# Two of sixteen pairs of PSUM copies: the second half of each moved from ScalarE to VectorE

## The chip, the cores and the metric

The kernel runs on one core of a Trainium2 chip. The metric is device time in microseconds (us) of one launch, the median of several runs. One run was also profiled: its instructions on TensorE (PE, with its weight loads as PEld), VectorE (DVE), ScalarE (ACT), GpSimd (POOL) and SyncE (SP, which issues the DMAs) are on a trace whose times count from the first instruction.

## The reference

A 2048 by 512 input goes through two blocks. The first normalizes each row, takes a real 2-D Fourier transform, multiplies it with a complex filter, transforms back and adds the input. The second normalizes again and applies a gated GELU layer of width 1376. All of it is float32.

```python
def _A_ref(x, w_r, w_i):
    X = jnp.fft.rfft2(x, axes=(-2, -1))
    X = X * (w_r + 1j * w_i)
    return jnp.fft.irfft2(X, s=(S, D), axes=(-2, -1))

h  = x + _A_ref(_layernorm(x), A_w_r, A_w_i)
g, u = _layernorm(h) @ w_gate, _layernorm(h) @ w_up
h2 = h + (_gelu(g) * u) @ w_down
```

## The kernel before

The transforms are matmuls with tables of sines and cosines. The kernel goes through four stages. The first (to about 30 us in the trace) loads and normalizes the rows and does a first transform. The second is the **filter stage**, about 30 to 74 us, and holds the change. The third transforms back along the other axis, adds the input and begins the gated layer. The fourth is the rest of the gated layer, and takes most of the time.

The filter stage works on 16 tiles of 128 partitions, t = 0 to 15. A tile passes through these steps, each named by the letter that stands for it in the string `SECOND`, which lists all steps of the stage in the order in which every engine gets its instructions:

- `o` (function `over_d`, line 420): four matmuls (L425, 128x128, float32; the trace shows each as two passes, so eight PE rows) write the tile's row spectra into two of the eight PSUM banks: banks 6 and 7 for tile 0, 0 and 1 for tile 1, 2 and 3 for tile 2, then 0 and 1 or 2 and 3. ScalarE then copies them to an SBUF tile `dp`, in two instructions (L429): partitions 0 to 63 first, then partitions 64 to 127 with the two banks' halves read in reverse. Each is 64x512 float32.
- `f` (`filtered`, line 431): two matmuls with weights `cfs` (L437, 128x256, four PE rows) read `dp` and write two banks, 4 and 5 for an even tile, 6 and 7 for an odd one. VectorE multiplies them with the filter's real and imaginary parts `wt` in three operations from PSUM (L443, L444, L445, here called the tile's **triple**), and GpSimd adds the two products (L453, L454) to `z`. SP then issues the load of the filter of tile t+8.
- `p` (`patch_w`): a ScalarE copy of 8 columns into the loaded filter tile (L472). The triple of the same tile waits for it.
- `b` (`back`): four matmuls with `z` as weights (L464, eight PE rows) write bank 0 or 1; at the end ScalarE copies that bank to `gh` (L469).
- `h`: a step of preparing weights of the gated layer. ScalarE rounds a piece (L156) and GpSimd subtracts it (L157).

The string begins `h p0 o0.6 o1.0 h h o2.2 h p1 f0 f1 p2 o3.0 o4.2 h f2 o5.0 h p3 p4 f3 o6.2 o7.0 h f4 o8.2 p5 f5 p6 p7 b0 o9.2 f6 p8 p9 b1 f7 o10.2 h p10 f8`. The number behind the point is the first PSUM bank. An engine works through its own instructions strictly in this order, and waits at each until its inputs are there and the place that it writes is free. So `o4` cannot start before ScalarE has read tile 2 out of banks 2 and 3, and `f(t)` not before VectorE has finished the triple of tile t-2, which reads the same two banks.

Of the kernel before, what the change touches and what calls it, by code (L numbers as in the profile page):

```python
# [15 lines left out]
AF = mybir.ActivationFunctionType  # L16
# [13 lines left out]
BY_POOL = (3,)  # L30

BY_THEN = (8, 12, 9)

START = """
f0 s0 g0 r0 n0 s1 c0 v0 g1 s2 m3 q3 r1 g2 f1 v1 n1 r2 m5 c1 q5 n2 c2 m7 c3 f2 s4 s6 g4 a0 b0 w7 g6 v2 q7 r4 n4 m9 c4
# [84 lines left out]
def kernel(  # L120
# [16 lines left out]
    pe, act, dve, pool = nc.tensor, nc.scalar, nc.vector, nc.gpsimd  # L137
# [97 lines left out]
    with (  # L235
# [182 lines left out]
        dps, zs = {}, {}  # L418

        def over_d(t, k):  # L420

            pd = ps[:, k : k + 2]
            for c, (e, q) in enumerate(((0, 0), (1, 1), (0, 1), (1, 0))):
                o = pd[:, e, q * NQ // 2 :][:, :P]
                pe.matmul(o, ts[:, t, c].rearrange("p x b k -> p (x b k)"), dfs[:, c], start=True, stop=True)  # L425
            pdv = pd[:, :, :NQ].rearrange("p e (s q) -> p s e q", s=2)[:, :, :, :P]
            dps[t] = w2.tile([P, 2, 2, P], F32, name="dp", bufs=5)
            for h, d in ((slice(0, 64), 1), (slice(64, P), -1)):
                act.activation(dps[t][h], pdv[h, ::d], AF.Copy)  # L429

        def filtered(t):
            dp, wt = dps.pop(t), wts.pop(t)
# [41 lines left out]
        with tc.manual_schedule(engines={et.PE, et.Activation, et.DVE, et.Pool}):  # L474
            prep = itertools.chain(raw0, load_gu(1, True))
            with tc.issue_after(kept.ins):
                for m, op in enumerate((ALU.add, ALU.subtract)):
                    pool.tensor_tensor(wh[:, :, m], ws[:, 0, :, m], ws[:, 1, :, m], op=op)
                act.activation(wh, wh, AF.Copy, scale=0.5)
            for _ in range(4):  # L480
                next(prep)
            rounded = 0
            for op in SECOND.split():
                name, *place = op.split(".")
                t = int(name[1:] or 0)
                if name == "h":
                    for _ in range(2 if rounded == 6 else 1):
                        next(prep, None)
                    rounded += 1
                elif name[0] == "o":  # L490
                    over_d(t, int(place[0]))
                elif name[0] == "f":
                    filtered(t)
                    if t + AHEAD < NT:
                        load_w(t + AHEAD)
                else:
                    (patch_w if name[0] == "p" else back)(t)
# [469 lines left out]
    def late(b):  # L967

        if b not in BY_THEN:

            with held("lo"):
                unfolded(b, row())
        yield
        xt = row()
        behind(nc.sync.dma_start(xt, x3[:, b]), pooled["raw"])
        py = ps[:, next(bank_67)]
        pe.matmul(py, mis[:, b], gh[:, b], start=True, stop=True)  # L977
        dve.scalar_tensor_tensor(gh[:, b], xt, mv[:, b, 0:1], py, op0=ALU.subtract, op1=ALU.add)  # L978
        for _ in stats2(b):
            pass  # L980
        yield
# [261 lines left out]
    lates = {2: (9, 13), 3: (10,), 4: (14,), 5: (11,), 6: (15,)}  # L1243
    ending = [late(b) for b in BY_THEN[:2]]
    for g in ending:
# [185 lines left out]
```

## Time and profile before

| what | value |
|---|---|
| median of 3 runs | 440.24 us (440.03 to 440.96) |
| the profiled execution's own time | 440.57 us |
| its span, first to last instruction | 438.3 us |
| PE busy | 432.5 us, 99% of the span |
| DVE busy | 311.2 us, 71% |
| ACT busy | 244.3 us, 56% |
| POOL busy | 314.9 us, 72% |
| copies L429 on ACT | 32 instructions of 0.591 to 0.593 us |

A row of the timeline gives the start in us, the length in us, the engine, the line, the operation, the tile written and the tiles read, the shapes, and how many instructions were merged into the row. Behind it, in brackets, stands how long the engine had been idle and what ended that. Matmuls are pipelined: a pass that runs 0.275 us is followed by the next one after 0.11 us, so the distance from the start of one PE row to that of the next tells more than the row's length. The waits list gives, for pairs of engine and line, the total idle time, how often, and the longest.

### The profile page before, as it was taken

The numbers are of one execution on the slowest core, as the hardware profiler recorded it, in microseconds if no ns is written. First come the engines' busy times: TensorE is split into PE (matmuls) and PEld (weight loads), VectorE is DVE, ScalarE is ACT, GpSimd is POOL, SyncE is SP. The second block draws the span as 40 slices with busy tenths as digits, with TensorE's granted clock in tenths as the row PEclk, the third lists the DMA queues.
The fourth block names the chain that finished last, engine by engine and source line by source line (L and its number), as shares of the span: only waits on it lengthen the run. The fifth ranks groups of instructions, "written<-read, shape, count | busy, mean of one in ns | idle before, by whom it ended". The sixth has DMA issues, their size and how long they took to land.

```text
span 438.3 us, 6627 instructions
## 1 busy us (share of the span) xinstructions
PE 432.5 (99%) x2275; PEld 367.0 (84%) x2275; DVE 311.2 (71%) x576; ACT 244.3 (56%) x505; POOL 314.9 (72%) x346
## 2 busy tenths in 40 slices
PE   8999999999999999999999999999999999999996
PEld 8998999789978777877888888888888888888885
DVE  5968976798764766368734579578677786687786
ACT  5989785799912442124432787376455653565640
POOL 6987897999958788658653944067879779787821
PEclk9999999999999999999999999999999999999999
DMA  8996904320032112112220203501212021200005
GB/s 265 404 414 118 357 12 150 134 72 25 1 120 97 49 55 91 48 49 72 72 73 24 73 25 120 169 15 58 73 48 73 28 69 49 72 25 2 0 1 194
DMA packets 23542, 41.60 MB, mean 95 GB/s; under 512 B 4178, under 2 KB 9810, under 8 KB 23380
## 3 DMA queue, kind: packets, MB, share of 16 engines
q1 hardware_dynamic: 23220, 40.92, 27.6%
q8 instruction: 18, 0.29, 0.3%
q10 hardware_dynamic: 288, 0.26, 0.2%
q14 instruction: 16, 0.13, 0.1%
HBM read 36.97 MB, written 4.20 MB: 94 GB/s over the span
## 4 chain that ended last, share of the span: by engine, by line
PE 92%; POOL 4%; DMA 1%; issue 1%; DVE 1%; ACT 0%; SPq 0%; DVEq 0%
PE ps L163 16%; PE ps L165 16%; PE ps L164 16%; PE ps L769 14%; PE ps L1108 11%; PE ps L425 4%; PE ps L530 3%; PE ps L437 3%; PE ps L464 3%; POOL pn L339 2%; POOL pn L338 2%; PE ps L869 2%; PE ps L977 1%; PE ps L1214 1%; DMA gh<-in_x 1%
## 5 line engine op out<-in xcount | busy, mean ns | idle before, releaser
L163 PE MATMUL ps<-cb,gu 128*128 128x512 f32 (+1 forms) x336 | 127.4, 379 | 0.0
L165 PE MATMUL ps<-cb,gu 128*128 128x512 f32 (+1 forms) x336 | 124.9, 372 | 0.0
L164 PE MATMUL ps<-cb,gu 128*128 128x512 f32 (+1 forms) x336 | 124.8, 371 | 0.0
L673 ACT ACTIVATE s<-ps 128x512 f32<-128x512 f32 (+1 forms) x72 | 40.3, 561 | 87.4 <-PE ps L165 87.2
L228 POOL TENSOR_TENSOR gu<-raw,gu 128x768 fp32r<-128x768 f32 (+1 forms) x42 | 61.4, 1481 | 29.9 <-DVE gu L223 15.5
L164 PEld LDWEIGHTS ps<-cb,gu 128*128 128x128 f32 x336 | 63.3, 188 | 11.8 <-issue 1.0
L163 PEld LDWEIGHTS ps<-cb,gu 128*128 128x128 f32 x336 | 63.3, 188 | 11.7 <-issue 1.0
L165 PEld LDWEIGHTS ps<-cb,gu 128*128 128x128 f32 x336 | 63.2, 188 | 11.1
L769 PE MATMUL ps<-wd,a 128*128 128x512 f32 x264 | 63.6, 393 | 0.0
L769 PEld LDWEIGHTS ps<-wd,a 128*128 128x128 f32 x264 | 49.2, 188 | 11.5 <-DVE gh L978 1.0
L682 DVE TENSOR_TENSOR ps<-ps,s 128x512 f32<-128x512 f32 (+1 forms) x48 | 31.2, 652 | 27.4 <-PE ps L165 25.3
L1115 DVE TENSOR_TENSOR gh<-ps,gh 128x512 f32<-128x512 f32 x66 | 44.2, 681 | 1.0 <-PE ps L1108 1.0
L679 ACT ACTIVATE s<-s 128x512 f32<-128x512 f32 (+1 forms) x48 | 28.5, 594 | 20.9 <-DVE s L676 20.9
L775 DVE TENSOR_TENSOR gh<-ps,gh 128x512 f32<-128x512 f32 x24 | 16.5, 689 | 27.0 <-PE ps L769 26.9
L676 DVE TENSOR_TENSOR s<-ps,s 128x512 f32<-128x512 f32 (+1 forms) x48 | 30.8, 641 | 5.8 <-PE ps L165 4.7
L511 POOL TENSOR_TENSOR wd<-wdr,wd 128x512 fp32r<-128x512 f32 x12 | 15.6, 1296 | 18.6 <-ACT wd L509 18.6
L676 DVE TENSOR_TENSOR ps<-ps,s 128x512 f32<-128x512 f32 (+1 forms) x24 | 15.7, 653 | 16.8 <-ACT s L673 16.6
L1021 POOL TENSOR_TENSOR t<-mis,t 128x768 fp32r<-128x768 f32 (+1 forms) x9 | 13.3, 1481 | 13.2 <-ACT t L1019 13.1
L688 ACT ACTIVATE a<-ps 128x512 fp32r<-128x512 f32 (+1 forms) x26 | 13.7, 532 | 15.6 <-DVE ps L682 15.6
L429 ACT ACTIVATE dp<-ps 64x512 f32<-64x512 f32 x32 | 18.9, 592 | 4.0 <-PE ps L425 3.6
L207 POOL TENSOR_TENSOR raw<-raw 128x256 f32<-128x256 f32 x16 | 11.8, 737 | 12.9 <-DMA raw<-in_wgu 11.2
L453 POOL TENSOR_TENSOR z<-t,t 128x520 f32<-128x520 f32 x15 | 19.4, 1296 | 2.1 <-DVE t L445 2.1
(183 smaller groups left out, 898.1 us busy)
## 6 DMA issues: line engine op xcount, KB each, us to landing
wt<-in_w SPq DMA_DIRECT2D x16, 520.0 KB, 7.1
raw<-in_wgu SPq DMA_DIRECT2D x32, 256.0 KB, 3.0
out<-gh SPq DMA_DIRECT2D x15, 256.0 KB, 2.0
gh<-in_x SPq DMA_DIRECT2D x7, 512.0 KB, 9.5
row<-in_x SPq DMA_DIRECT2D x12, 256.0 KB, 2.7
wdr<-in_wd SPq DMA_DIRECT2D x12, 256.0 KB, 2.6
mis<-in_wd SPq DMA_DIRECT2D x10, 256.0 KB, 2.6
a<-in_wgu SPq DMA_DIRECT2D x8, 256.0 KB, 3.1
```

The source lines that it names most:

```text
L163: pe.matmul(o, lh, rh, start=(i == 0 and not onto), stop=False, skip_group_check=True)
L164: pe.matmul(o, lh, rl, start=False, stop=False, skip_group_check=True)
L165: last = pe.matmul(o, ll, rh, start=False, stop=(i == n - 1), skip_group_check=True)
L228: pooled["lo"] = pool.tensor_tensor(r[:, 1, m], t[:, m], r[:, 0, m].bitcast(F32), op=ALU.subtract)
L453: eng.tensor_tensor(z[:, :, first], t1[:, :, first], t2[:, :, first], op=ALU.add)
L673: return lambda: act.activation(to, a, AF.Copy)
L676: return lambda: dve.tensor_tensor(to, a, b, op=ALU.add)
L679: return lambda: act.activation(g, g, AF.Gelu_apprx_tanh)
L682: return lambda: dve.tensor_tensor(u, u, g, op=ALU.mult)
L769: pe.matmul(o, parts_of[tiles.index((0, f))][:, ha, i // 4, r], wds[f][:, hw, c], start=start, stop=stop)
L1108: pe.matmul(ps[:, k], w[:, hw], a[ha], start=start and hw + ha == 0, stop=hw == 1, skip_group_check=True)
L1115: by.tensor_tensor(to, o, to, op=ALU.add)
```

## The change

For tiles 0 and 1 alone, the second of the two copies out of PSUM (partitions 64 to 127) is a `tensor_copy` on VectorE. The first copy of these two tiles and both copies of the other fourteen stay on ScalarE.

```diff
+COPIED_BY_VECTOR = (0, 1)
...
             for h, d in ((slice(0, 64), 1), (slice(64, P), -1)):
-                act.activation(dps[t][h], pdv[h, ::d], AF.Copy)
+                if t in COPIED_BY_VECTOR and d < 0:
+                    dve.tensor_copy(dps[t][h], pdv[h, ::d])
+                else:
+                    act.activation(dps[t][h], pdv[h, ::d], AF.Copy)
```

The changed program has five lines more, so L429 becomes L434 on ScalarE and L432 on VectorE, L437 becomes L442, L443 to L445 become L448 to L450, L472 becomes L477 and L156 becomes L158. Names in brackets are what an instruction waits for: an engine's counter, or a DMA queue (DMAHW).

ScalarE at the head of the filter stage, before (`gu` is the rounding of step `h`, `wt` the patch `p`, `dp` the copies):

```order
L472 ACTIVATE wt<-wh 128x4x2 [waits DMAHW2_49,Activation_49]
L429 ACTIVATE dp<-ps 64x512 [waits DVE_49,PE_49]
L429 ACTIVATE dp<-ps 64x512
L429 ACTIVATE dp<-ps 64x512 [waits DVE_49,PE_49]
L429 ACTIVATE dp<-ps 64x512
L156 ACTIVATE gu<-raw 128x256
L156 ACTIVATE gu<-raw 128x256 [waits Pool_49]
L429 ACTIVATE dp<-ps 64x512 [waits PE_49]
L429 ACTIVATE dp<-ps 64x512
L156 ACTIVATE gu<-raw 128x256 [waits DMAHW1_49]
```

The same place now:

```order
L477 ACTIVATE wt<-wh 128x4x2 [waits DMAHW2_49,Activation_49]
L434 ACTIVATE dp<-ps 64x512 [waits DVE_49,PE_49] x2
L158 ACTIVATE gu<-raw 128x256
L158 ACTIVATE gu<-raw 128x256 [waits Pool_49]
L434 ACTIVATE dp<-ps 64x512 [waits PE_49]
L434 ACTIVATE dp<-ps 64x512
L158 ACTIVATE gu<-raw 128x256 [waits DMAHW1_49]
```

Four copies ahead of the two `gu` have become two, the first halves of tiles 0 and 1. Everything behind them stands as it did.

VectorE at the same place, before (`t` are the products of the triples):

```order
L383 COPY ts<-ps 128x16x4x4 [waits PE_49]
L412 TENSOR_SCALAR mv<-m_113 128x6
L443 TENSOR_TENSOR t_494<-ps,wt 128x520 [waits DVE_49,DMAHW2_49,PE_49,Activation_49]
L444 SCALAR_TENSOR_TENSOR t_495<-ps,wt 64x520
L445 TENSOR_TENSOR t_495<-ps,wt 64x520
```

And now:

```order
L385 COPY ts<-ps 128x16x4x4 [waits PE_49]
L414 TENSOR_SCALAR mv<-m_113 128x6
L432 COPY dp<-ps 64x512 [waits DMAHW5_49,DMAHW0_49,Activation_49]
L432 COPY dp<-ps 64x512 [waits Activation_49]
L448 TENSOR_TENSOR t_494<-ps,wt 128x520 [waits DMAHW2_49,PE_49]
L449 SCALAR_TENSOR_TENSOR t_495<-ps,wt 64x520
L450 TENSOR_TENSOR t_495<-ps,wt 64x520
```

The two copies stand ahead of the first triple. Each waits for ScalarE's counter: the value is the one reached when ScalarE has finished the first half of the same tile, not merely when PE has finished the matmuls. The two halves of a tile therefore still follow one another. On PE, the `f` matmuls of tiles 0 and 1 now wait for VectorE's counter where they waited for ScalarE's.

## The prediction

> **What bounds the kernel now.** I read first the page's chain of waits (the work that ended last, by engine), then the waits list for 30 to 75 us.
>
> ```profile
> PE 92%; POOL 4%; DMA 1%; issue 1%; DVE 1%; ACT 0%; SPq 0%; DVEq 0%
> ...
> PEld ps L425 <- ACT dp L429: 0.8, 4, 0.2
> ```
>
> PE carries the chain almost alone, so only time in which PE stands still, or starts later, can be gained. In the filter stage it stands still for the copies of the change (`dp`, L429): four times ahead of an `o`. The list shows only idle time above the overlap of the passes, so I read the timeline of PE row by row (start, length, line, passes).
>
> ```profile
> 30.29 2.92 PE L425 MATMUL ps<-dfs,ts 128*128 128x128 f32 x24
> ...
> 33.05 2.01 PE L437 MATMUL ps<-dp,cfs 128*128 128x256 f32 x8
> 34.89 2.16 PE L425 MATMUL ps<-dfs,ts 128*128 128x128 f32 x16
> 36.89 1.03 PE L437 MATMUL ps<-dp,cfs 128*128 128x256 f32 x4
> 37.76 1.16 PE L425 MATMUL ps<-dfs,ts 128*128 128x128 f32 x8
> 38.75 1.03 PE L437 MATMUL ps<-dp,cfs 128*128 128x256 f32 x4
> 39.62 2.18 PE L425 MATMUL ps<-dfs,ts 128*128 128x128 f32 x16
> 41.63 1.03 PE L437 MATMUL ps<-dp,cfs 128*128 128x256 f32 x4
> 42.51 1.16 PE L425 MATMUL ps<-dfs,ts 128*128 128x128 f32 x8
> 43.51 1.03 PE L437 MATMUL ps<-dp,cfs 128*128 128x256 f32 x4
> 44.37 1.05 PE L464 MATMUL ps<-cis,z 128*128 128x128 f32 x8
> 45.39 1.16 PE L425 MATMUL ps<-dfs,ts 128*128 128x128 f32 x8
> 46.39 1.03 PE L437 MATMUL ps<-dp,cfs 128*128 128x256 f32 x4
> ...
> 49.01 1.05 PE L425 MATMUL ps<-dfs,ts 128*128 128x128 f32 x8
> 49.99 1.13 PE L437 MATMUL ps<-dp,cfs 128*128 128x256 f32 x4
> ...
> 54.50 1.06 PE L425 MATMUL ps<-dfs,ts 128*128 128x128 f32 x8
> 55.40 1.03 PE L437 MATMUL ps<-dp,cfs 128*128 128x256 f32 x4
> 56.26 1.05 PE L464 MATMUL ps<-cis,z 128*128 128x128 f32 x8
> ...
> 68.62 5.76 PE L464 MATMUL ps<-cis,z 128*128 128x128 f32 x48
> ```
>
> An undisturbed `o` (eight L425 passes) takes 0.90 us from start to start (54.50 to 55.40), an `f` 0.86 (55.40 to 56.26); `b` has eight passes as well and is taken like `o`. Against that: f0+f1 took 34.89-33.05 = 1.84, 0.12 too long; o3+o4 2.00, 0.20 too long; o5 0.99, 0.09; o6+o7 2.01, 0.21; o8 1.00, 0.10; b0 1.02, 0.12; o9 1.00, 0.10; o10, up to the start of f8, 0.98, 0.08. That is 1.02 us of hidden stalls before f8 at 49.99. From there to 68.62 lie eight `f`, five `o` and eight `b`: 6.88+11.70 = 18.58 of 18.63 us. So behind f8 PE runs without gaps worth naming, and everything before f8 decides. What PE waited for is seen in ScalarE's timeline, and in a stretch of it by engine (columns: length, then busy us of PE, PEld, DVE, ACT, POOL).
>
> ```profile
> 31.46 2.41 ACT L429 ACTIVATE dp<-ps 64x512 f32<-64x512 f32 x4 [0.25 <-PE ps L425]
> 33.90 0.72 ACT L156 ACTIVATE gu<-raw 128x256 fp32r<-128x256 f32 x2
> 34.64 1.20 ACT L429 ACTIVATE dp<-ps 64x512 f32<-64x512 f32 x2
> 35.86 0.42 ACT L156 ACTIVATE gu<-raw 128x256 fp32r<-128x256 f32 x1
> 36.19 0.30 ACT L472 ACTIVATE wt<-wh 128x8 f32<-128x8 f32 x2
> 36.51 2.42 ACT L429 ACTIVATE dp<-ps 64x512 f32<-64x512 f32 x4
> 38.95 0.42 ACT L156 ACTIVATE gu<-raw 128x256 fp32r<-128x256 f32 x1
> ...
> 40.94 0.30 ACT L472 ACTIVATE wt<-wh 128x8 f32<-128x8 f32 x2
> ...
> 45.36 0.41 ACT L472 ACTIVATE wt<-wh 128x8 f32<-128x8 f32 x3
> ```
>
> ```profile
> 39.00:44.00 5.00, 5.00 (x35) 4.42 (x34) 4.39 (x7) 4.84 (x11) 4.50 (x7) 1.00 0.73 171
> ```
>
> ScalarE is the engine that is late: four copies in a row from 31.46, then `h`, and from 36.51 it works almost without a break (4.84 of 5 us). VectorE comes next; its rows for the first operation of tiles 0, 1, 3, 5 and 6, and the last operation of tile 6:
>
> ```profile
> 34.17 0.70 DVE L443 TENSOR_TENSOR t<-ps,wt 128x520 f32<-128x520 f32 x1 [3.34 <-ACT dp L429]
> ...
> 36.42 0.70 DVE L443 TENSOR_TENSOR t<-ps,wt 128x520 f32<-128x520 f32 x1
> ...
> 41.22 0.70 DVE L443 TENSOR_TENSOR t<-ps,wt 128x520 f32<-128x520 f32 x1 [0.53 <-POOL gu L157]
> ...
> 45.67 0.70 DVE L443 TENSOR_TENSOR t<-ps,wt 128x520 f32<-128x520 f32 x1 [0.17 <-issue]
> ...
> 47.82 0.70 DVE L443 TENSOR_TENSOR t<-ps,wt 128x520 f32<-128x520 f32 x1
> ...
> 49.25 0.69 DVE L445 TENSOR_TENSOR t<-ps,wt 64x520 f32<-64x520 f32 x1
> ```
>
> Triples that follow one another are 2.15 apart (45.67 to 47.82), and a triple ends 2.12 after its start (49.25+0.69 = 49.94). f8 starts 0.05 later, at 49.99: it writes the banks that triple 6 reads, so **f8 waits for VectorE**. VectorE's chain from 34.17 to 49.94 is 15.77 long, and seven triples back to back would need 6 x 2.15 + 2.12 = 15.02. The rest, 0.75, was lost where a triple waited. Triple 3 (idle 0.53) started right behind the patch p3, on ScalarE at 40.94 and done 0.20 later; the name in the bracket is of work that had ended by then, and I take p3. Triple 5 started 0.31 behind the start of p5 (45.36).
>
> **The change, part by part.** Two copies of 0.60 leave ScalarE and two come to VectorE. The trace has a copy from PSUM on VectorE only with 256 elements:
>
> ```profile
> L383 DVE COPY ts<-ps x1: 425/425/425, 29.8 to 29.8; 128x256 f32<-128x256 f32 x1
> ```
>
> The operations of the triples, 520 elements from PSUM, take 0.70. In line between 0.425 for 256 and 0.70 for 520, a copy of 512 takes **0.69 us**; I take that, and keep 0.43 and 0.70 as ends.
>
> *Tile 0.* ScalarE's half ends at 31.46+0.59 = 32.05. VectorE's copy waits for that; with 0.05 for the semaphore it runs from 32.10 to 32.79, where ScalarE's ended at 32.65. It is 0.14 later, and free: f0 could not start before PE had finished o2, which it did at 33.05. The cover is 0.2 us, and VectorE itself was idle (3.34 us ahead of 34.17). Behind the waiting copies VectorE has triple 0, which needs f0's result anyway and stays at 34.17. The filter load that SP issues behind triple 0 stays too.
>
> *Tile 1.* The third eight of the 24 passes end at 33.21, so o1's end at 32.31. ScalarE is now free and copies the first half at 32.35 to 32.95, VectorE the second at 33.00 to 33.69. f1, straight behind f0 at 33.91, finds it done. The 0.12 at f1 is gained and o3 starts at 34.77.
>
> *ScalarE.* The two `gu` run 32.95 to 33.69 (0.74, as 33.90 to 34.64), tile 2's copies to 34.91 (1.22), the next `gu` with p1 and p2 to 35.56 (0.65). Tile 3's copies need o3, done 34.77+1.06 = 35.83 (a row of o5, 1.16, less its 0.10 stall); so they start at 35.87, not 36.51. **ScalarE is 0.64 ahead**, the rest of its 1.2 us is lost in waiting for o3. From there it stays 0.64 ahead as long as PE is in time: tile 6's copies at 40.62 need o6, done 40.51 below; tile 8's at 43.50 need o8, done 43.17. So p3 starts at 40.30, p5 at 44.72.
>
> *PE.* o4 at 35.67 finds its banks copied (34.91): 0.20 gained. f2 36.57, o5 37.43 (banks copied by 37.08): 0.09 gained. f3 could start at 38.33, but its banks are read by triple 1, which now starts at 34.17+2.15 = 36.32, ends at 38.44, and lets f3 go at 38.49, with another 0.10 inside the stalled group, as o5 showed. Here **VectorE takes over the wait**, and most of the lead is gone for the moment: 38.75 before. Then o6 39.45, o7 40.35 (copied by 39.97), f4 41.25, o8 42.11 (41.84), f5 43.01, b0 43.87 (43.06), o9 44.77 (44.70, the tightest), f6 45.67, o10 48.29, and f8 could start at 49.19.
>
> *VectorE.* Triple 2 at 38.47, triple 3 at 40.62 (p3 done 40.50), triple 4 at 42.77, triple 5 behind p5 at 44.72+0.31 = 45.03, triple 6 at 47.18, done 49.30. f8 starts at 49.35 instead of 49.99: **0.64 us earlier**, and its inner stall stays.
>
> Behind f8 the stalls are small and each is a wait for work that PE itself started, so I carry the 0.64 through. The span becomes 438.3-0.64 = 437.7, the profiled execution's time 440.57-0.64 = 439.93. That execution lay 0.33 above the median; from the median I get 440.24-0.64 = **439.6 us**. If the copy takes 0.43, f0 still waits for PE and nothing changes; at 0.70 neither.
>
> **Rivals.**
> 1. *Hidden anyway.* If triple 3 does not move, because p3 or the triple waited for something else than ScalarE's turn, or if the lead is eaten in the later stages, little is left. With triple 3 fixed at 41.22, triple 4 is at 43.38, 5 at 45.53, 6 at 47.68, done 49.80; f8 at 49.85, gain 0.14: 440.1 us. For it: the bracket at 41.22 names another engine. Against: ScalarE had no break before p3. Chance 0.24.
> 2. *More.* VectorE's chain is at its shortest with 15.02: f8 at 34.17+15.02+0.05 = 49.24, and the 0.10 inside f8 gone as well. Gain 0.85: 439.4 us. It needs ScalarE 0.1 further ahead at p5, and nothing shows where from. Chance 0.12.
> 3. *Slower: the copies sit ahead of triple 0 in VectorE's queue.* If a copy takes D instead of 0.69, the second ends at 32.10+2D (from D = 0.9), and triple 0 starts behind it. f8 then starts 0.04+15.02+0.05 after that, and is later than 49.99 once 2D exceeds 2.78, so from D = 1.39 on; at D = 1.8 f8 starts at 50.81, 0.82 late: 441.1 us. Against it: no VectorE operation of this size from PSUM takes over 0.70 here. Chance 0.04.
> 4. *The copies wait for GpSimd.* GpSimd works back to back at this place:
>
> ```profile
> 31.68 0.73 POOL L215 TENSOR_TENSOR raw<-raw 128x256 f32<-128x256 f32 x1
> 32.37 0.73 POOL L157 TENSOR_TENSOR gu<-raw,gu 128x256 fp32r<-128x256 f32 x1
> ```
>
> If such a copy could not run beside GpSimd, the first would start at 33.10, behind the second row. With 0.69 it ends at 33.79, f0 starts at 33.84 instead of 33.05, triple 0 at 34.96, and f8 at 50.03: 440.3 us, no gain. Against it: triple 0 ran at its usual 0.70 from 34.17, and GpSimd's rows beside other VectorE work keep their 0.73. Chance 0.05.
>
> The Trainium skill has such a rule in SBUF — State Buffer, section "SBUF: two separate sides": a VectorE operation that uses both its SBUF ports and a GpSimd operation exclude one another for the whole instruction. But in VectorE: DVE Perf Modes, section "Why PSUM operands drop a tier", it says that a float32 operand in PSUM keeps an operation at one element per cycle, since there is one read port to PSUM; then no second port is taken and the lock does not apply. The row of L383, 425 ns for 256 elements, agrees with the single rate. By the second page the sum above holds, by the first alone rival 4 would.
>
> **How the numbers follow.** The forecast has 0.55. About 0.2% (0.88 us) is what a measurement of this kernel can tell from no change, and the forecast lies inside, as do rivals 1 and 4. Faster by over 0.2% means below 439.36: rival 2 lies at that edge and gives half of its 0.12, and the forecast gives 0.16 for steps sized too small and for runs that vary (440.03 to 440.96 above): 0.22. Slower than 441.12: half of rival 3, and 0.04 for variation and a later stage that answers badly: 0.06. Within: 0.72. The range goes from 439.0, rival 2 with 0.4 for variation, to 440.5, which takes in rivals 1 and 4; rival 3 stays out.
>
> **What would show it.** In the trace of the changed kernel: the two VectorE copies near 0.69 us, starting right behind ScalarE's halves; f0 still at 33.05 and triple 0 at 34.17; ScalarE's copies of tile 3 at about 35.9; no stall at o4, o5, o7 and o8, and a new one at f3 behind VectorE; triple 3 at about 40.6, f8 at about 49.35, and the first L530 row 0.64 before its old place. The prediction is wrong if a copy takes over 0.85, which would move f0; if triple 3 stays where it was; or if f8 is early and the end of the span is not.

## The result

| | before | after |
|---|---|---|
| median of 11 runs each | 440.24 us (439.92 to 440.96) | 439.29 us (439.12 to 439.69) |
| profiled execution, its span | 440.57, 438.3 us | 439.26, 437.0 us |
| first `o` to `f8` in the trace | 19.70 us | 19.04 us |
| first `o` to the first L530 row (now L535) | 44.16 us | 43.50 us |

The ratio is 0.998, with a 95% interval from 0.9973 to 0.9988. The kernel became 0.95 us faster, 0.22%; the prediction had 439.6, 0.64 us faster, and a range from 439.0 to 440.5. In the trace the filter stage is 0.66 us shorter. So the stage did what was worked out, and about 0.3 us of the gain came from elsewhere; the experiments look for it.

PE after the change, from the timeline (start, length, line, passes):

```profile
29.97 2.92 PE L427 MATMUL ps<-dfs,ts 128*128 128x128 f32 x24
32.72 1.89 PE L442 MATMUL ps<-dp,cfs 128*128 128x256 f32 x8
34.45 1.95 PE L427 MATMUL ps<-dfs,ts 128*128 128x128 f32 x16
36.23 1.03 PE L442 MATMUL ps<-dp,cfs 128*128 128x256 f32 x4
37.10 1.05 PE L427 MATMUL ps<-dfs,ts 128*128 128x128 f32 x8
38.12 1.13 PE L442 MATMUL ps<-dp,cfs 128*128 128x256 f32 x4
39.08 1.95 PE L427 MATMUL ps<-dfs,ts 128*128 128x128 f32 x16
...
49.01 1.13 PE L442 MATMUL ps<-dp,cfs 128*128 128x256 f32 x4
...
73.47 3.84 PE L535 MATMUL ps<-dis,gh 128*128 128x128 f32 x32
```

The stage begins 0.32 us earlier than in the trace of before, at 29.97 and not at 30.29. So places are compared from the first `o` on: `f0` 2.75 behind it in both, `f1` no longer late (f0 and f1 take 1.73 us together and not 1.84), `o3` and `o4` 1.78 instead of 2.00. From `o5` (37.10) to `f3` (38.12) it is 1.02 where an undisturbed `o` takes 0.90: the new stall of 0.12 ahead of `f3`. The row of `f3` is 1.13 us long, 0.10 longer than that of an undisturbed `f`, as that of `f8` is in both traces.

ScalarE and VectorE at the same place:

```profile
31.14 0.59 ACT L434 ACTIVATE dp<-ps 64x512 f32<-64x512 f32 x1 [0.26 <-PE ps L427]
32.03 0.59 ACT L434 ACTIVATE dp<-ps 64x512 f32<-64x512 f32 x1 [0.30 <-PE ps L427]
32.52 0.71 ACT L158 ACTIVATE gu<-raw 128x256 fp32r<-128x256 f32 x2
33.13 1.18 ACT L434 ACTIVATE dp<-ps 64x512 f32<-64x512 f32 x2
...
35.54 2.41 ACT L434 ACTIVATE dp<-ps 64x512 f32<-64x512 f32 x4 [0.58 <-PE ps L427]
```

```profile
31.76 0.69 DVE L432 COPY dp<-ps 64x512 f32<-64x512 f32 x1 [1.26 <-ACT dp L434]
32.65 0.69 DVE L432 COPY dp<-ps 64x512 f32<-64x512 f32 x1 [0.20 <-ACT dp L434]
33.79 0.70 DVE L448 TENSOR_TENSOR t<-ps,wt 128x520 f32<-128x520 f32 x1 [0.44 <-PE ps L442]
...
40.25 0.70 DVE L448 TENSOR_TENSOR t<-ps,wt 128x520 f32<-128x520 f32 x1
...
46.84 0.70 DVE L448 TENSOR_TENSOR t<-ps,wt 128x520 f32<-128x520 f32 x1
...
48.26 0.69 DVE L450 TENSOR_TENSOR t<-ps,wt 64x520 f32<-64x520 f32 x1
```

A copy takes 0.69 us on VectorE and 0.59 on ScalarE. VectorE's two copies lie in time in which it was idle before. ScalarE begins tile 3's copies 35.54-29.97 = 5.57 behind the first `o`; before it was 36.51-30.29 = 6.22. Triple 3 starts without waiting, 10.28 instead of 10.93 behind the first `o`, and `f8` follows the end of triple 6 (48.26+0.69 = 48.95) by 0.06, before by 0.05.

### The profile page after: what moved, and what is told of

The parts are those of the page before. It is cut to its first block, busy times and chain, and to the rows that moved or that the text cites. A ratio compares the mean times of both kernels' runs of the same rounds, so it can differ in the third digit from the quotient of the medians.

```text
span 437.0 us, 6628 instructions
## 1 busy us (share of the span) xinstructions
PE 431.5 (99%) x2275; PEld 367.4 (84%) x2275; DVE 312.6 (72%) x578; ACT 242.8 (56%) x503; POOL 314.4 (72%) x346
## 4 chain that ended last, share of the span: by engine, by line
PE 98%; issue 0%; DVE 0%; ACT 0%; POOL 0%; DVEq 0%; POOLq 0%
PE ps L165 16%; PE ps L166 16%; PE ps L167 16%; PE ps L774 14%; PE ps L1113 11%; PE ps L374 5%; PE ps L427 3%; PE ps L535 3%; PE ps L442 3%; PE ps L469 3%; PE ps L176 2%; PE ps L874 2%; PE ps L982 1%; PE ps L1219 1%; PE ps L568 1%; PE ps L574 1%
## 5 line engine op out<-in xcount | busy, mean ns | idle before, releaser
L434 ACT ACTIVATE dp<-ps 64x512 f32<-64x512 f32 x30 | 17.7, 591 | 4.8 <-PE ps L427 4.5
```

## The experiments

Each run has its own runs of before on the same chip beside it; their median was 440.21 us for the first four and 440.22 for the others. "Stage" is the distance from the first L427 row of PE to its first L535 row; before and the two kernels with before's copies have 44.14 to 44.16.

### The five lines alone

The flag is there and no tile is chosen, so that all copies are on ScalarE.

```diff
-COPIED_BY_VECTOR = (0, 1)
+COPIED_BY_VECTOR = ()
```

> The changed source with an empty list of tiles: the same instructions as before the change, only on other line numbers. The trace of the change showed the expected 0.65 us between the start of o0 and the start of f8 (19.70 before, 19.04 after), yet the medians differ by 0.95. Theory (the other 0.3 us are differences between executions and have nothing to do with the copies): the median is that of the kernel before within 0.2 us, the distance o0 to f8 is 19.7, and the start of o0 lies somewhere between 29.9 and 30.4. Rival (the added lines alone shift the program and its first 30 us): 0.3 us faster than before, o0 at about 30.0.

Measured: 440.22 us, ratio 1.0002 (0.9993 to 1.0011), `f8` 19.69 behind the first `o`, stage 44.14. The lines by themselves change nothing. The theory's other half, that the 0.3 us are mere differences between executions, is not tested by this run; the later ones speak against it.

### One tile at a time

```diff
-COPIED_BY_VECTOR = (0, 1)
+COPIED_BY_VECTOR = (0,)
```

> Only tile 0's second copy on VectorE. Theory (the gain is ScalarE's lead at tile 3's copies, as far as o3 lets it be used): tile 1's copies are done by ScalarE at 32.35 to 33.55 in the times of the trace before, two gu to 34.29, tile 2's copies to 35.51, gu and patches to 36.16, tile 3's copies from 36.20 where they began at 36.51; lead 0.31, o0 to f8 19.39 us. Rival (the gain is the wait ahead of f1 alone, 0.12): o0 to f8 19.58.

```diff
-COPIED_BY_VECTOR = (0, 1)
+COPIED_BY_VECTOR = (1,)
```

> Only tile 1's second copy on VectorE. It can begin only at 33.32, ends at 34.01, so f1 waits about as long as before (0.15 and 0.10 inside); o3 is then done at 36.08 and tile 3's copies begin at 36.12, not 36.51. Theory: lead 0.39, o0 to f8 19.31 us. Rival (the wait ahead of f1 alone is the gain): it stays, so o0 to f8 remains 19.70.

Measured: with tile 0 alone `f8` at 19.36 and 439.62 us, ratio 0.9987 (0.9979 to 0.9996); with tile 1 alone `f8` at 19.29 and 439.83 us, ratio 0.9990 (0.9981 to 0.9999). Both stages end where the theory of the turns on ScalarE put them, 0.03 and 0.02 us from it, and far from the rivals. ScalarE's copies of tile 3 show it, tile 0 alone first (its first `o` at 29.97), then tile 1 alone (30.11):

```profile
35.86 2.42 ACT L434 ACTIVATE dp<-ps 64x512 f32<-64x512 f32 x4
```

```profile
35.93 2.41 ACT L434 ACTIVATE dp<-ps 64x512 f32<-64x512 f32 x4 [0.50 <-PE ps L427]
```

Tile 0 alone gets ScalarE there 5.89 behind the first `o` without a break, tile 1 alone 5.82 after a wait of 0.50 for PE: there ScalarE has time to spare and PE is late, because `f1` still waits for a copy. But the times stand the wrong way round: tile 0 alone gains less in the stage (0.33 against 0.41) and more in the time (0.59 against 0.38).

### The missing quarter: a pause of VectorE near the end

PE's rows of the lines alone and of tile 0 alone, laid against each other, keep one distance of about 0.4 us, to within 0.04, from 73 us to 429 us; then it grows to 0.64. With tile 1 alone it doesn't grow. What is late at 429 us is seen on VectorE, which stands still a little earlier, both in before and in the lines alone. First before, its waits between 410 and 438 us and three rows of VectorE; then the changed kernel at the same place.

```profile
DVE a L1034 <- issue: 0.5, 1, 0.5
```

```profile
422.62 0.68 DVE L1115 TENSOR_TENSOR gh<-ps,gh 128x512 f32<-128x512 f32 x1
423.80 0.69 DVE L1034 TENSOR_TENSOR a<-ps,a 96x512 fp32r<-96x512 f32 x1 [0.50 <-issue]
...
429.35 0.68 DVE L1115 TENSOR_TENSOR gh<-ps,gh 128x512 f32<-128x512 f32 x1
```

```profile
421.59 0.68 DVE L1120 TENSOR_TENSOR gh<-ps,gh 128x512 f32<-128x512 f32 x1
422.40 0.69 DVE L1039 TENSOR_TENSOR a<-ps,a 96x512 fp32r<-96x512 f32 x1
...
427.98 0.68 DVE L1120 TENSOR_TENSOR gh<-ps,gh 128x512 f32<-128x512 f32 x1
```

The subtraction of 96 rows starts 1.18 us behind the operation ahead of it in before, and 0.81 us in the changed kernel. In before VectorE's row at 429.35 therefore ends at 430.03, and PE, which waits for that row, starts at 430.08. The wait in the list of before from 74 us on, then PE in before and in the changed kernel:

```profile
PEld ps L1108 <- DVE gh L1115: 0.4, 1, 0.4
```

```profile
429.29 0.84 PE L1214 MATMUL ps<-a,wd 128*128 128x512 f32 x3
430.08 0.97 PE L1108 MATMUL ps<-a,t 128*128 128x512 f32 x3
430.89 0.39 PE L1214 MATMUL ps<-a,wd 128*128 128x512 f32 x1
```

```profile
428.27 0.84 PE L1219 MATMUL ps<-a,wd 128*128 128x512 f32 x3
428.95 0.84 PE L1113 MATMUL ps<-a,t 128*128 128x512 f32 x3
429.63 0.62 PE L1219 MATMUL ps<-a,wd 128*128 128x512 f32 x2
```

Three passes take 0.68 us from start to start. In before the step to L1108 takes 0.79 and the step behind it 0.81: the pause costs PE 0.11+0.13 = 0.24 us. In the changed kernel the same VectorE operation ends at 428.66, 0.29 ahead of the matmuls that need it, and nothing is lost.

Why is the pause gone? In before nothing released the waiting row ("issue"). The idea: VectorE pauses at a fixed place in its row of instructions. One instruction more ahead of it, a copy, say, puts that place one instruction earlier, among the instructions that only wait for semaphores. Those run ahead of the arithmetic, and there a pause is hidden. The trace's rows of these instructions, which the views leave out, are spaced by 0.10 us in the kernel with the lines alone; in the changed kernel one of these distances, from 421.10 to 421.55, is 0.45. The test keeps all copies on ScalarE and issues one small VectorE instruction more at the start of the program, which writes a constant a second time:

```diff
-COPIED_BY_VECTOR = (0, 1)
+COPIED_BY_VECTOR = ()
...
+    dve.memset(eps, EPS)
```

> The copies as before the change (none on VectorE), and one tiny memset more at the head of VectorE's program (the same constant written twice). Around 423.4 us VectorE stands still for 0.40 us for nothing that the profile shows, ahead of the 96x512 subtraction, in the three programs with 726 VectorE rows in the trace (before, none, tile 1), and not in those with 727 to 729 (tile 0, the change, three tiles), which are 0.2 to 0.3 us faster than their filter stages explain. Theory (a pause at a fixed place in VectorE's row of instructions; one instruction more moves it onto a wait that runs ahead): filter stage as before (o0 to f8 19.70), no pause ahead of the subtraction, from the first L530 pass to PE's last about 359.4 us and not 359.6 to 359.8, median about 439.97. Rival (the pause goes with the copies' times, or is chance): median 440.2.

Measured: 439.95 us against 440.22, ratio 0.9994 (0.9985 to 1.0003), with the filter stage unchanged (`f8` 19.70, stage 44.15). The interval holds 1, so the times alone don't prove it; the trace shows the step. Laid against each other, PE's rows of this kernel and of the lines alone keep their distance to within 0.01 us from 300 to 429 us, and then this kernel gains 0.24. First the kernel with the lines alone, then the one with the additional instruction:

```profile
422.26 0.68 DVE L1120 TENSOR_TENSOR gh<-ps,gh 128x512 f32<-128x512 f32 x1
423.42 0.69 DVE L1039 TENSOR_TENSOR a<-ps,a 96x512 fp32r<-96x512 f32 x1 [0.48 <-issue]
```

```profile
422.31 0.68 DVE L1121 TENSOR_TENSOR gh<-ps,gh 128x512 f32<-128x512 f32 x1
423.12 0.69 DVE L1040 TENSOR_TENSOR a<-ps,a 96x512 fp32r<-96x512 f32 x1
```

With one instruction more the distance is 0.81, as in the changed kernel. The way from the first L535 row (L536 here) to the last matmul is 359.47 us, where the lines alone need 359.63: 0.16 less and not 0.24, since 0.06 us were lost between 250 and 300 us and some hundredths before. VectorE has 726 rows in the traces of before, of the lines alone and of tile 1 alone, and all three pause ahead of the subtraction; in the traces with 727 to 730 rows it does not. Tile 1 alone has one copy more and one instruction that only waits less, and so keeps 726. That is why it was slower than tile 0 alone.

The place can be counted. Taken in the program's order, the row that starts late is the 704th row of VectorE in nine of the ten traces: the subtraction itself in the three with 726 rows, and one of the four waiting instructions ahead of it, late by 0.35 to 0.37 us, in six others (in the kernel with each copy twice it would be the first of the four, where no pause can be told from the wait ahead of it). The 64th row, too, starts 0.44 to 0.47 us behind the one ahead of it in all ten traces, although in the kernel with the additional memset it is another instruction. So the pause goes by the count.

What goes with the pause is seen in the DMA view: a packet on a queue of kind "instruction" follows it. First before, between 424 and 425 us in 40 slices, then the changed kernel, between 422 and 423:

```profile
DMA  0000000000000000090000000000000000000000
...
q14 instruction: 1, 0.01, 2.6%
```

```profile
DMA  0000000090000000000000000000000000000000
...
q14 instruction: 1, 0.01, 2.3%
```

In before the packet starts between 424.43 and 424.45, some 0.64 us behind the end of the pause (423.80). In the changed kernel it starts between 422.20 and 422.23, some 0.66 behind the end of the hidden one (421.55). It moved with the pause. The view does not say for which engine a packet is. The Trainium skill, in Runtime: NRT & Kernel Launch, section "Instruction fetch mechanics", says that an engine's instructions are fetched in blocks of 256 by the engine's own queue, and that crossing a block's end costs one bump of that queue, mostly hidden. The size differs here: the packets of q14 are of 8 KB (in the page of before 16 packets, 0.13 MB), where that section gives 16 KiB for a block. By its figures 8 KB would be 128 instructions, which is an estimate; from the 64th row to the 704th it is five times 128. So a crossing fits, and "mostly" is what this case shows: 0.4 us, hidden in one program and 0.24 us of the time in the next. That the crossing causes the pause is inferred from the two going together; no run took the fetch away. And as the packet starts only behind the pause, VectorE cannot have waited for its data: what it does in these 0.4 us stays open.

### A third tile

```diff
-COPIED_BY_VECTOR = (0, 1)
+COPIED_BY_VECTOR = (0, 1, 2)
```

> Tile 2's second copy on VectorE as well. Theory (VectorE's chain of triples from triple 0 to triple 6 takes 15.02 us at best and ends at f8): the third copy stands ahead of triple 0 in VectorE's queue, waits for ScalarE's half of tile 2 and ends at 35.02, so triple 0 starts at 35.06 and not 34.17; f8 at 50.13, o0 to f8 19.83 us, some 0.8 us slower than the change and about level with the kernel before. Rival (each copy taken from ScalarE is worth 0.33 us): o0 to f8 18.72, faster than the change.

Measured: 439.98 us, ratio 0.9997 (0.9988 to 1.0006), `f8` at 19.67 and the stage 44.13. VectorE and ScalarE here:

```profile
33.84 0.69 DVE L432 COPY dp<-ps 64x512 f32<-64x512 f32 x1 [0.40 <-ACT dp L434]
34.57 0.70 DVE L448 TENSOR_TENSOR t<-ps,wt 128x520 f32<-128x520 f32 x1
```

```profile
33.23 0.58 ACT L434 ACTIVATE dp<-ps 64x512 f32<-64x512 f32 x1
```

The third copy stands in VectorE's queue ahead of triple 0, as expected: the triple starts 34.57-30.07 = 4.50 behind the first `o`, where it could have started at 3.82, and the whole gain is gone. I had it 0.27 later still, since I had taken ScalarE's half of tile 2 to start later; it starts at 3.16. `f8` was expected at 19.83; the rival's 18.72 is far off. What is left of the time, 0.23 us faster than before, agrees with the pause of VectorE, which this kernel does not have at that place either, but the ratio's interval holds 1. (Its profiled execution took 440.86 and was not a typical one; the stage is read from it, the time is not.)

### Each copy twice

Both VectorE copies are issued twice, so that a copy costs double; the result of the copy stays the same.

```diff
                 if t in COPIED_BY_VECTOR and d < 0:
                     dve.tensor_copy(dps[t][h], pdv[h, ::d])
+                    dve.tensor_copy(dps[t][h], pdv[h, ::d])
```

> Each of the two VectorE copies is issued twice, so that the pair stands for a copy of 1.39 us. Theory (cover of 0.2 us ahead of f0, then VectorE's queue is the bound): in the times of the trace before, tile 0's second copy ends at 33.50, f0 starts at 33.55 and not 33.05, tile 1's at 34.88, f1 at 34.93 and triple 0 at 34.92 and not 34.17; ScalarE's copies of tile 3 at 37.0, triple 5 at 46.2, f8 at 50.5: o0 to f8 20.2 us, 1.15 longer than with single copies. Rival (the copies are hidden in VectorE's idle time of 3.3 us): o0 to f8 19.0.

```profile
31.84 0.69 DVE L432 COPY dp<-ps 64x512 f32<-64x512 f32 x1 [1.26 <-ACT dp L435]
32.57 0.69 DVE L433 COPY dp<-ps 64x512 f32<-64x512 f32 x1
33.19 0.69 DVE L432 COPY dp<-ps 64x512 f32<-64x512 f32 x1
33.91 0.69 DVE L433 COPY dp<-ps 64x512 f32<-64x512 f32 x1
34.63 0.70 DVE L449 TENSOR_TENSOR t<-ps,wt 128x520 f32<-128x520 f32 x1
```

Measured: 440.41 us, ratio 1.0007 (0.9998 to 1.0016), `f8` at 20.20 as expected, the stage 44.65: 0.50 us longer than before. Four copies stand ahead of triple 0, which starts 4.58 behind the first `o`. So the slower rival is real: had a copy cost VectorE 1.4 us, the change would have lost in the stage. Rival 3 had put the break-even at 1.39 us; it counted the delay of triple 0 alone. Here `f0` and `f1` start late as well (3.32 and 4.70 behind the first `o`, before 2.75 and 3.63), `o3` with them, and ScalarE waits 1.73 us for `o3` before tile 3's copies. The time is only 0.2 longer than before, which agrees with the hidden pause, though here too the interval holds 1.

### Filling the stalls that are left

After the change PE still stands ahead of `f3` (0.23 with the longer second half), `o9` (0.13) and `f8` (0.20), waiting for VectorE twice and ScalarE once. Two other orders put matmuls that are ready into these places. The first starts `o6` ahead of `f3` and `b2` ahead of `f8`:

```diff
-... h p3 p4 f3 o6.2 o7.0 ... b1 f7 o10.2 h p10 f8 h b2 o11.2 ...
+... h p3 p4 o6.2 f3 o7.0 ... b1 f7 o10.2 h p10 b2 f8 h o11.2 ...
```

> The change, and in the string of steps o6 stands ahead of f3, and b2 ahead of f8, so that PE has other work where it now waits for triples 1 and 6. Theory (these two waits, 0.23 and 0.20, are what is left of VectorE's bound): from o0 to the first L530 pass 43.07 us instead of 43.50; median 438.9. Rival (VectorE's chain then holds up a later step): 43.5.

The second also puts `b1` ahead of `o9`:

```diff
-... p6 p7 b0 o9.2 f6 p8 p9 b1 f7 o10.2 h p10 f8 h b2 o11.2 ...
+... p6 p7 b0 b1 o9.2 f6 p8 p9 f7 o10.2 h p10 b2 f8 h o11.2 ...
```

> As the run before, and b1 ahead of o9, where PE waits 0.13 for tile 8's copies. Theory: another 0.13, from o0 to the first L530 pass 42.95 us, median 438.75. Rival (f6 comes 0.9 later, so triple 6 starts 0.1 late and the rest follows): 43.1 or more.

Measured: the first 439.27 us, ratio 0.9978 (0.9969 to 0.9987), stage 43.30; the second 439.36 us, ratio 0.9981 (0.9972 to 0.9989), stage 43.47. The first stage is 0.20 shorter than that of the change, half of what was hoped: stalls of 0.12 and 0.22 remain at `o6` and `o9`. And the time is no better. The second order delays `o9` and `f6` and with them triples 6 and 7, as its rival had it (43.1 or more). `f8` no longer waits, but the list of waits between 30 and 75 us shows the stall come back one step later, at `f9`, which writes the banks that triple 7 reads (the longer of the two; `f9` starts 1.15 behind `o11`, undisturbed 0.89):

```profile
PEld ps L442 <- DVE t L450: 0.5, 2, 0.3
```

Where did the 0.20 of the first order go? To the start of the third stage. One row each of GpSimd, of SyncE's queue and of VectorE from the timeline of the changed kernel, then of the first order:

```profile
71.61 0.72 POOL L159 TENSOR_TENSOR gu<-raw,gu 128x256 fp32r<-128x256 f32 x1
...
73.28 1.83 SPq L808 DMA_DIRECT2D a<-in_x  x4
...
78.62 1.61 DVE L884 SCALAR_TENSOR_TENSOR a<-a,mv,ps 128x512 f32<-128x512 f32 x2 [0.15 <-ACT t L879]
```

```profile
72.23 0.73 POOL L159 TENSOR_TENSOR gu<-raw,gu 128x256 fp32r<-128x256 f32 x1
...
73.90 1.82 SPq L808 DMA_DIRECT2D a<-in_x  x4
...
78.66 1.41 DVE L884 SCALAR_TENSOR_TENSOR a<-a,mv,ps 128x512 f32<-128x512 f32 x2 [0.55 <-DMA a<-in_x]
```

GpSimd's last subtraction of a step `h` (L159) starts 0.62 us later. SyncE waits for such a subtraction ahead of a load of weights (L202), and the four loads of the input that are queued behind go out 0.62 later too. VectorE, which adds the input, waits 0.55 us for the first of them and starts no earlier than in the changed kernel, and PE's next matmuls wait for VectorE. At 77 us PE is 0.36 us ahead of the changed kernel (0.20 of the stage and 0.16 of the first stage), at 80 us 0.13. So these 0.23 us take back the whole gain of the order; which step of the new order makes GpSimd late was not tried.

### The sum over all runs

Two terms account for the times: the change of the stage (against 44.15), and 0.24 us if the pause is hidden.

| kernel | stage | pause | sum | measured against before |
|---|---|---|---|---|
| the lines alone | 0.0 | stays | 0.0 | +0.01 |
| tile 0 alone | -0.33 | hidden | -0.57 | -0.59 |
| tile 1 alone | -0.41 | stays | -0.41 | -0.38 |
| the change (tiles 0, 1) | -0.65 | hidden | -0.89 | -0.95 |
| tiles 0, 1, 2 | -0.02 | hidden | -0.26 | -0.23 |
| one instruction more | 0.0 | hidden | -0.24 | -0.27 |
| each copy twice | +0.50 | hidden | +0.26 | +0.19 |
| first order | -0.85 | hidden | -1.09 | -0.95 |
| second order | -0.68 | hidden | -0.92 | -0.86 |

All but the first order lie within 0.07 us of their sum; the first order is 0.14 off, on the side of what its third stage gives back. The interval of each ratio is about 0.4 us wide to either side, so no row proves its sum by itself; what counts is that they agree, and that the traces show both terms.

## Why the prediction was right, and what it missed

- *A copy takes 0.69 us on VectorE.* Right: 694 ns. The line through 256 and 520 elements held, and the copies ran beside GpSimd at full speed (its rows from 31.35 and 32.04, 0.73 each as before), so rival 4 is out: the first started 0.03 us behind ScalarE's half.
- *f0 and triple 0 don't move.* Right: 2.75 behind the first `o` in both traces, the triple 3.82 instead of 3.88.
- *ScalarE is 0.64 ahead from tile 3 on.* Right: 0.65, after a wait for PE (0.58), as the working had it. ScalarE reached tile 2's copies another 0.24 earlier than worked out (33.13; the sum gives 33.69, less the 0.32), since `gu` rows behind a copy overlap with it; the wait for `o3` swallowed that.
- *VectorE takes over the wait at f3.* Right; and `o9`, named as the tightest, did start 0.03 late and lost 0.10 inside, which the wait of `f8` for VectorE covered. At `f3` the only pair of this kind left in the waits list is

```profile
PEld ps L442 <- DVE t L450: 0.2, 1, 0.2
```

- *Triple 3 starts behind p3, f8 0.64 earlier.* Right: triple 3 is 0.65 earlier and `f8` 0.66. The bracket that named GpSimd at triple 3 was misleading, as assumed; rival 1 is out. Rival 2 needed the copies ahead at `p5` as well; triple 5 still waited (0.17), and the stage stayed at 0.66. So it is luck that rival 2's time, 439.4, lies nearer to the measured 439.29 than the forecast.
- *The slower rival* needed more of VectorE's time ahead of triple 0. Two copies fit; a third, or each twice, showed its price: the gain of 0.65 gone, or 0.50 lost. Its sum was too mild: it had no loss at 1.39 us for a copy, where 0.50 was measured. And what was said against it, that no VectorE operation of this size from PSUM takes over 0.70, holds in the filter stage only: operations with three operands (128x512) take 0.74 to 0.75 later in the trace of before.
- *"Behind f8 I carry the 0.64 through."* Here the sum was incomplete. The 0.64 was carried through, to the first L535 row (0.66) and on, but the change has a second effect which no term had: two VectorE instructions more in the program moved a pause of 0.4 us, 390 us later, to a place where it costs nothing. That is 0.24 of the missing 0.31, and the stage gave 0.02 more than worked out. In the trace of before it stood as a row of waits, `DVE a L1034 <- issue: 0.5`, which I did not read, since I looked at the waits of the filter stage alone. The remaining 0.05 is not resolved. So it is partly luck that the time lies inside the range: its lower end, 439.0, was drawn from rival 2 and from variation, and neither has to do with this pause.
- *The chances.* By the medians the time lies a hair over the bound of 0.2% (0.95 us against 0.88), on the side that had 0.22, and the ratio's interval reaches to both sides of it. The 0.72 for "within" was given to a gain of 0.64; with the pause in the sum, 0.88, it would have been an even choice.
- The spans differ by 1.3 us and not by 0.95, because the profiled execution of before was 0.33 over its median. The first `o` at 30.29 and 29.97 puts 0.32 of it into the first stage, which the change does not touch.

## What to carry to other kernels

Follow the lead of the relieved engine through each wait to the place where PE last waits, and count the queue of the engine that takes the work over: two copies were free there, three cost all that was gained. When the gain is a fraction of a microsecond, read also the waits marked "issue" far behind the change, since an instruction more or less on an engine can move them onto or off the path. A control that adds an instruction and none of the effect (here one repeated constant) tells the two apart.

## What was not expected of the hardware

- VectorE pauses for about 0.40 us at a place fixed by the count of its instructions (the 704th row of its trace), 0.64 to 0.66 us ahead of an instruction packet on a DMA queue in the two traces shown. On arithmetic it cost PE 0.24 us; on instructions that only wait, nothing.
- A group of matmuls that starts late loses about 0.1 us more inside: `f3` 1.13 instead of 1.03 us long, the three passes at 430.08 0.97 instead of 0.84. So these two stalls, of 0.12 and 0.11 us, cost PE about twice what shows ahead of the group. The loss inside did not grow with the wait: with three tiles `f2` started 0.41 late and was 1.13 long as well.
